# Attention backward, last pass: who requests the weight slabs of wq and wo, when, and into which buffers

## The chip, the cores and the metric

The kernel runs on one core of a Trainium2 chip. The metric is the device time of one execution, in microseconds (us); less is better. A core has a matrix engine (PE, TensorE, whose weight loads are listed as PEld), a vector engine (DVE, VectorE), an activation engine (ACT, ScalarE), a general one (POOL, GpSimd) and SyncE (SP), which here only requests transfers. Transfers between device memory and the on-chip buffers run on 16 transfer (DMA) engines. Each engine works through its own list of instructions in order. A transfer is requested by an instruction on one engine's list, and each requesting engine has its own queue of transfers.

## What is computed

The reference runs four layers on one token and then the gradient of all of it:

```python
x = x + _A_ref(_layernorm(x, axis=-1), A_k_cache, A_v_cache, A_wq, A_wo)
x = x + _B_ref(_layernorm(x, axis=-1), B_w1, B_b1, B_w2, B_b2)
x = x + _A_ref(_layernorm(x, axis=-1), A_k_cache, A_v_cache, A_wq, A_wo)
x = x + _B_ref(_layernorm(x, axis=-1), B_w1, B_b1, B_w2, B_b2)
```

`_A_ref` is attention with 32 query heads in 4 groups over a cache of 65536 positions of 128 numbers for each group (k and v, bf16, 67 MB each); q is x times wq (1024 x 4096), and the result goes through wo (4096 x 1024). `_B_ref` is a dense layer with a squared ReLU. Both attention layers use the same cache and weights. The outputs are the last x and the gradients with respect to x, k, v, wq, wo, w1, b1, w2 and b2. The gradients of k and v are as large as the caches: 134 MB that have to be written.

## The kernel before, in words

The kernel goes through the caches four times: two forward passes, a backward pass for the second attention layer, and a last pass that does the backward of the first attention layer and writes the gradients of k and v for both layers together. Only this last pass is touched.

**The last pass** (`attn_bwd4`) goes through 256 *items*, each of 8 columns of 128 cache positions: head groups 3, 2, 1, 0, 64 items each, in units of four items. A unit needs one 1 MB block of v and one of k. `pipeline` issues, for item i, the stages of different cache columns: v is turned by PE (`vT`, L1354), multiplied (`vS`, L1391), outer products make the gradients of v and k (`outer16`, PE at L1435), which ACT or DVE copy into a store buffer (`evac`, L161 and L164), and k is multiplied (`k8`, L1466). At the end of each item `bg.step` lets a background job do one step.

**Background jobs.** A job is a generator. `Background.step` gives each item's one step to the first *urgent* job; if that one yields "wait", the *normal* jobs (outer products for the weight gradients) get the step. Urgent are six jobs that multiply a vector with the rows of a weight matrix for one head group: `g_dO` (with wo, for groups 2, 1, 0, before the group's first v block is used) and `g_dn` (with wq, for groups 3, 2, 1, after the group's end). Called dO2, dO1, dn3, dO0, dn2, dn1 here, in the order in which they run, they start at items 16, 72, 102, 136, 166 and 202 of the background's count. Each needs 8 rows of 1024 columns for every partition, in two *slabs* of 1 MB, each with four of the rows. `g_rowdots` first spreads the vector (four steps, `g_bcast_vec`, L568 and L570), and then does one row a step: DVE multiplies (L596), and ACT sums the row of the step before (L585). `slabs` requests a slab when the loop comes to it (L459), so the second one only after the first has been used; the job then yields "wait" four times ahead of the first slab's rows and eight times ahead of the second's. In the last pass ACT requests the slabs of wq and SP those of wo.

**Buffers.** The arena has 20 buffers of 1 MB. Eight hold the exponentials of both layers for four groups, and two of them come free at the end of each group (`E_done`). A set `RING` marks the buffers that are meant for stores: two at the start of the pass, up to `NRING` = 5 soon after, and two more at the end of each group. `take_one` gives a store (`fill` true) the ring buffer that has been free for longest, and a load or a slab the one outside the ring that has been free for longest. Which buffer is used is settled when the program is written; at run time a request waits on its engine until the last user of that buffer is done. Loads of k and v (`kv8`, L361, L366) are written at the item that first uses them, and requested by SP, which has nothing else to do and so runs ahead of the other engines as far as the buffers let it. Stores (L1441 and others) are requested by POOL.

What decides on a buffer is this:

```python
if PS["pass4"]:
    mine = [i for _, i in by_age if (i in RING) == fill]
    i = mine[0] if mine else by_age[0][1] if fill else by_age[-1][1]
    del FREE[i]
    return i
```

The functions that the change touches, and those that call them:

Of the kernel before, what the change touches and what calls it, by code (L numbers as in the profile page):

```python
# [10 lines left out]
BF = mybir.dt.bfloat16  # L11
F32 = mybir.dt.float32
ACTF = mybir.ActivationFunctionType
ALU = mybir.AluOpType
AX = mybir.AxisListType
PSUM = bass.MemoryType.PSUM
P = 128
# [3 lines left out]
def kernel(  # L21
# [24 lines left out]
    nc = tc.nc  # L46
# [6 lines left out]
    R = HQ // G  # L53
    F = B_w1.shape[1]
    DC, FC = D // P, F // P
# [10 lines left out]
    TLEAD = 2  # L66
    STORE_STEPS = 5
    WAIT_STEPS = 5
    NSLOT = 12
    NWT = 6  # L70
    NKEEP = [8, 7, 7]
    NRING = 5
# [9 lines left out]
    PS = {}  # L82
# [62 lines left out]
    def add_load(act=0.0, dve=0.0, pe=0.0):  # L145
        load["act"] += act
        load["dve"] += dve
        load["pe"] += pe
# [289 lines left out]
    def f_rows_of(W):  # L438
        return W.rearrange("(s p j) n -> p s j n", p=P, j=4)

    def slabs(name, load, nk, kper, ncols, ahead=1, flat=False):
        pend = deque()
        ks = deque(range(0, nk, kper))

        def fetch():
            k = ks.popleft()
            i = None
            if ks and flat and NOW["wide"] and not odd_one():
                i = take_pair()
            if i is None:  # L450
                kn = min(kper, nk - k)
                sl = Slot(name)
            else:
                kn = min(2 * kper, nk - k)
                ks.popleft()
                sl = Slot(name, at=i, both=True)
            v = sl.t[:, 0:kn * ncols].rearrange("p (k n) -> p k n", n=ncols)
            queue = nc.scalar if PS["pass4"] and name == "s_wq" else nc.sync
            queue.dma_start(out=v, in_=load(k, kn))  # L459
            pend.append((k, kn, sl, v))  # L460

        def gen():
            while ks or pend:
                while ks and len(pend) < ahead:
                    fetch()
                k, kn, sl, v = pend.popleft()
                for kk in range(kn):
                    NOW["slab"] = sl
                    yield k + kk, v[:, kk, :]
                sl.over = True  # L470
                if not sl.users:
                    sl.free()
        g = gen()
        g_fetch = [fetch for _ in range(ahead)]
        return g, g_fetch
# [5 lines left out]
            f()  # L481
        return g

    def wq_slabs(g, ahead=1):
        v = rows_of(A_wq)
        return slabs("s_wq", lambda k, kn: v[:, k:k + kn, g * 1024:(g + 1) * 1024], DC, 4, 1024, ahead, True)

    def wo_slabs(g, ahead=1):
        v = rows_of(A_wo)
        return slabs("s_wo", lambda k, kn: v[:, g * R + k:g * R + k + kn, :], R, 4, 1024, ahead, True)  # L490

    def wo_runs(g):

        v = A_wo[g * 1024:(g + 1) * 1024, :].rearrange("(p k) n -> p k n", k=8)
        return slabs("s_wo", lambda k, kn: v[:, k:k + kn, :], R, 4, 1024, 1, True)[0]

    def w1_slabs(ahead=1):
        v = rows_of(B_w1)
# [58 lines left out]
    def g_bcast_vec(vcol, nj):  # L557
        pt = ps_mv([nj, P], F32)
        nc.tensor.transpose(pt[:, :], vcol, ident_f[:, :])
        yield  # L560
        rows = tmp.tile([32, P], BF, name="bc_rows")
        nc.vector.tensor_copy(out=rows[0:nj, :], in_=pt[:, :])
        vbc = mvs.tile([P, nj * P], BF, name="vbc", tag="vbc", bufs=1)
        yield
        for j0 in range(0, nj, 4):
            pg = ps_gg() if PS["pass4"] else ps_tr([P, 512], F32)
            for jj in range(4):
                nc.tensor.matmul(pg[:, jj * P:(jj + 1) * P], lhsT=ident_b[0:nj, j0 + jj:j0 + jj + 1].to_broadcast([nj, P]),  # L568
                                 rhs=rows[0:nj, :], start=True, stop=True)
            nc.scalar.copy(out=vbc[:, j0 * P:(j0 + 4) * P], in_=pg[:, 0:512])  # L570
            add_load(act=0.6)
            yield
        return vbc

    def g_rowdots(slab_it, nk, vcol, nj, finish, name):
        n = nj * P
        y = vec.tile([P, nk], F32, name=name)
        nc.gpsimd.memset(y[:], 0.0)
        vbc = None
        due = None  # L580
        steps = 8 if PS["pass4"] else WAIT_STEPS

        def total(t, kc):
            def f():
                nc.scalar.activation(out=t[:, :], in_=t[:, :], func=ACTF.Copy, accum_out=y[:, kc:kc + 1])  # L585
            return f
        for kc, slab in slab_it:
            if vbc is None:
                vbc = yield from g_bcast_vec(vcol, nj)
                for _ in range(steps - WAIT_STEPS + 1):  # L590
                    yield "wait"
            elif kc % 4 == 0:
                for _ in range(steps):
                    yield "wait"
            t = mvs.tile([P, n], BF, name="mv_t", tag="mv_t", bufs=2)
            nc.vector.tensor_tensor(out=t[:, :], in0=slab, in1=vbc[:, :], op=ALU.mult)  # L596
            add_load(dve=0.1 + n * 0.00054, act=0.42 + n * 0.00083)
            if due is not None:
                due()
            due = total(t, kc)  # L600
            yield
        due()
        yield
        r = finish(y[:, :])
        if r is not None:
            yield from r
        yield
# [308 lines left out]
    def gsl(g):  # L916
        return slice(g * R, (g + 1) * R)
# [10 lines left out]
    def g_wo(L, xacc, g, ps=ps_bg, it=None):  # L928
        def fin(p):
            nc.vector.tensor_tensor(out=xacc[:], in0=xacc[:], in1=p, op=ALU.add)  # L930
        if it is not None:
            yield from g_mv(it, R, 8, lambda kc: L["oTb"][:, g * R + kc:g * R + kc + 1], ps, fin)
            return
        each = tmp.tile([P, R, 8], BF, name="run_each", bufs=1)
        nc.vector.tensor_tensor(out=each[:, :, :], in0=L["oTb"][:, gsl(g)].unsqueeze(2).to_broadcast([P, R, 8]),
                                in1=eighth[:, :].unsqueeze(1).to_broadcast([P, R, 8]), op=ALU.mult)
        yield
        pt = ps_mv([P, R, 8])
        nc.tensor.matmul(pt[:, :, :].rearrange("p r k -> p (r k)"), lhsT=to_runs[:, :, :].rearrange("p a b -> p (a b)"),
                         rhs=each[:, :, :].rearrange("p r k -> p (r k)"), start=True, stop=True)  # L940
        yield
        own = tmp.tile([P, 8, R], F32, name="run_own", bufs=1)
        nc.vector.tensor_tensor(out=own[:, :, :], in0=pt[:, :, :].rearrange("p r k -> p k r"),
                                in1=M8[:, :].unsqueeze(1).to_broadcast([P, 8, R]), op=ALU.mult)
        oruns = tmp.tile([P, 8], F32, name="run_o")
        nc.vector.tensor_reduce(out=oruns[:], in_=own[:, :, :], axis=AX.X, op=ALU.add)
        orunb = tmp.tile([P, 8], BF, name="run_ob")
        nc.vector.tensor_copy(out=orunb[:], in_=oruns[:])
        yield
        yield from g_mv(wo_runs(g), R, 8, lambda kc: orunb[:, kc:kc + 1], ps, fin)  # L950


    def dO_finish(L, g):
# [18 lines left out]
    def g_dO(L, dx, g):  # L972
        def fin(y):
            each = tmp.tile([P, R, 8], F32, name="run_own", bufs=1)
            nc.vector.tensor_tensor(out=each[:, :, :], in0=y.unsqueeze(1).to_broadcast([P, R, 8]),
                                    in1=M8[:, :].unsqueeze(2).to_broadcast([P, R, 8]), op=ALU.mult)
            yield
            pt = ps_mv([P, R, 8], F32)
            nc.tensor.matmul(pt[:, :, :].rearrange("p r k -> p (r k)"), lhsT=from_runs[:, :, :].rearrange("p a b -> p (a b)"),
                             rhs=each[:, :, :].rearrange("p r k -> p (r k)"), start=True, stop=True)  # L980
            yield
            own = tmp.tile([P, R, 8], F32, name="run_own", bufs=1)
            nc.vector.tensor_tensor(out=own[:, :, :], in0=pt[:, :, :], in1=eighth[:, :].unsqueeze(1).to_broadcast([P, R, 8]), op=ALU.mult)
            back = tmp.tile([P, R], F32, name="run_o")
            nc.vector.tensor_reduce(out=back[:], in_=own[:, :, :], axis=AX.X, op=ALU.add)
            yield
            yield from dO_finish(L, g)(back[:, :])
        yield from g_rowdots(wo_runs(g), R, dx[:], DC, fin, "%s_dO%d" % (L["name"], g))


    def dn_finish(dn, first):
        def fin(y):
            if first:
                nc.vector.tensor_copy(out=dn[:], in_=y)
            else:
                nc.vector.tensor_tensor(out=dn[:], in0=dn[:], in1=y, op=ALU.add)
        return fin

    def g_dn(L, dn, g, first):
        yield from g_rowdots(wq_slabs(g)[0], DC, L["dqT"][:, gsl(g)], R, dn_finish(dn, first), "%s_dn%d" % (L["name"], g))  # L1000


    ACT_KT = (3, 13, 15)
# [1054 lines left out]
```

## Time and profile before

| | before |
|---|---|
| runs, median (lowest to highest of 3) | 1934.7 us (1932.66 to 1939.24) |
| profiled execution, its own time | 1936.54 us |
| its span, first to last instruction | 1934.7 us |
| bytes moved, mean rate over the span | 787.62 MB, 407 GB/s |
| busy share of the span: PE, DVE, ACT, POOL | 82%, 61%, 54%, 7% |
| 1 MB stores: requests, median from issue to landing | 149, 15.2 us |
| 1 MB slabs of wq by ACT: requests, median to landing | 8, 25.3 us |

The time and the span of the profiled execution differ by 1.8 us, which lie around the first and the last instruction. The profile lists, for each engine, what it was busy with, how long it sat idle and which instruction or transfer ended the wait; for the transfer engines, what they moved in each stretch of time. "Idle before" is the idle time just before an instruction. A request is on SP's, ACT's or POOL's list, and its landing is when the last byte has arrived.

### The profile page before, as it was taken

What the parts mean: (1) busy time and instruction counts of PE and PEld (TensorE: products, weight loads), DVE (VectorE), ACT (ScalarE), POOL (GpSimd) and SP (SyncE); (2) the same over time, 40 slices, a digit from 0 to 9 for tenths busy, and PEclk for the clock granted to TensorE, in tenths of its full rate; (3) what the DMA queues carried; (4) which work ended last, traced back from release to release, by engine and by line L of the source; (5) the groups of instructions that cost most, each with busy time, mean ns of one, the idle gap of its engine ahead of it and who ended that gap; (6) DMA issues with size and microseconds to landing.
All of it is one profiled execution on the core that took longest, in us unless ns stands there. A gap on an engine that the chain in (4) does not pass through costs nothing. (4 is left out here: it accounts for less than half of the span.)

```text
span 1934.7 us, 66770 instructions
## 1 busy us (share of the span) xinstructions
PE 1595.9 (82%) x30099; PEld 1303.7 (67%) x30099; DVE 1171.8 (61%) x2448; ACT 1044.5 (54%) x1619; POOL 143.4 (7%) x325
## 2 busy tenths in 40 slices
PE   6878788688778878978787888888978979789796
PEld 6878778678777778877777885555555555456463
DVE  5655555255555554645454576777867777667685
ACT  3434333345333545445363465666867677667676
POOL 0000000000000000000000002111211111111111
PEclk9989998799999998999899999898988889788896
DMA  9999999999999999999999997999999999999997
GB/s 394 426 428 424 427 429 416 403 420 415 428 425 428 429 414 327 376 426 429 425 426 422 404 366 285 425 424 386 424 425 423 424 402 407 393 403 416 421 419 301
DMA packets 107148, 787.62 MB, mean 407 GB/s; under 512 B 9440, under 2 KB 16622, under 8 KB 42222
## 3 DMA queue, kind: packets, MB, share of 16 engines
q1 hardware_dynamic: 78558, 609.26, 76.2%
q0 software_dynamic: 24080, 165.70, 20.5%
q10 hardware_dynamic: 4224, 8.39, 1.1%
q8 instruction: 235, 3.85, 0.7%
q14 instruction: 51, 0.42, 0.1%
HBM read 617.62 MB, written 165.69 MB: 405 GB/s over the span
## 5 line engine op out<-in xcount | busy, mean ns | idle before, releaser
L164 DVE COPY kt<-ps_tr 128x1024 bf16<-128x1024 bf16 x736 | 504.9, 688 | 434.6 <-PE ps_tr L1031 240.3
L161 ACT CAST arena<-ps_gg 128x1024 bf16<-128x1024 f32 x457 | 444.4, 1012 | 204.1 <-PE ps_gg L1435 136.3
L1031 PE MATMUL ps_tr<-ident_b,arena 128*128 128x128 bf16 x3840 | 312.4, 227 | 49.7 <-DMA arena<-in_A_k_cache_dram 37.0
L161 ACT COPY kt<-ps_tr 128x1024 bf16<-128x1024 bf16 x180 | 188.3, 1051 | 190.7 <-PE ps_tr L1225 108.9
L164 DVE CAST arena<-ps_gg 128x1024 bf16<-128x1024 f32 (+2 forms) x186 | 222.1, 1194 | 88.5 <-PE ps_gg L1435 51.1
L1031 PEld LDWEIGHTS <-arena 128*128 128x128 bf16 x3840 | 235.3, 102 | 58.6 <-DMA arena<-in_A_k_cache_dram 39.6
L1132 PE MATMUL ps_acc<-arena 128*128 128x64 bf16 (+4 forms) x4096 | 204.2, 196 | 46.4 <-DMA arena<-in_A_v_cache_dram 29.4
L1435 PE MATMUL ps_gg<-GG,xt 64*128 64x512 bf16 x1024 | 216.8, 420 | 19.5 <-ACT arena L161 8.8
L1354 PE MATMUL ps_tr<-ident_b,arena 128*128 128x128 bf16 x1824 | 181.2, 235 | 30.3 <-DMA arena<-in_A_v_cache_dram 16.4
L1049 PE MATMUL ps_sc<-L_qpad,kt 128*128 128x64 bf16 (+7 forms) x3584 | 183.5, 194 | 17.9 <-issue 10.9
L1114 ACT ACTIVATE arena<-S_sb,L_negm 128x128 bf16<-128x128 f32 x256 | 165.1, 1005 | 60.3 <-DVE L_negm L1099 60.3
L1225 PE MATMUL ps_tr<-ident_b,arena 128*128 128x128 bf16 x2032 | 161.7, 224 | 40.7 <-DMA arena<-in_A_v_cache_dram 39.0
L1132 PEld LDWEIGHTS <-arena 128*128 128x128 bf16 x4096 | 159.4, 101 | 52.4 <-DMA arena<-in_A_v_cache_dram 33.0
L1354 PEld LDWEIGHTS <-arena 128*128 128x128 bf16 x1824 | 120.7, 105 | 88.4 <-issue 68.7
L1049 PEld LDWEIGHTS <-kt 128*128 128x128 bf16 x3584 | 153.3, 100 | 21.8 <-issue 11.7
L1225 PEld LDWEIGHTS <-arena 128*128 128x128 bf16 x2032 | 122.6, 100 | 46.8 <-DMA arena<-in_A_v_cache_dram 41.3
L1466 PEld LDWEIGHTS <-arena 128*128 128x128 bf16 x2048 | 91.1, 101 | 63.1 <-DMA arena<-in_A_k_cache_dram 32.2
L1114 ACT ACTIVATION_READ_ACCUMULATOR arena<-S_sb,L_negm 128x1 f32 x256 | 128.0, 500 | 0.0
L1391 PEld LDWEIGHTS <-kt 128*128 128x128 bf16 x1824 | 85.2, 102 | 50.3 <-issue 48.7
L1391 PE MATMUL ps_sc<-DOB,kt 128*128 128x64 bf16 (+3 forms) x1824 | 118.2, 198 | 0.1
L1466 PE MATMUL ps_acc<-X,arena 128*128 128x64 bf16 (+3 forms) x1536 | 94.8, 197 | 26.3 <-DMA arena<-in_A_k_cache_dram 26.3
L585 ACT ACTIVATE mv_t<-mv_t 128x1024 bf16<-128x1024 bf16 x96 | 102.0, 1064 | 21.6 <-DVE mv_t L596 21.5
(319 smaller groups left out, 2102.8 us busy)
## 6 DMA issues: line engine op xcount, KB each, us to landing
arena<-in_A_k_cache_dram SPq DMA_DIRECT2D x82, 2048.0 KB, 21.4
arena<-in_A_v_cache_dram SPq DMA_DIRECT2D x79, 2048.0 KB, 20.7
out_dram<-arena POOLq DMA_DIRECT2D x149, 1024.0 KB, 15.2
arena<-in_A_v_cache_dram SPq DMA_DIRECT2D x84, 1024.0 KB, 12.6
arena<-in_A_k_cache_dram SPq DMA_DIRECT2D x84, 1024.0 KB, 12.8
arena<-in_A_wo_dram SPq DMA_DIRECT2D x22, 1024.0 KB, 13.9
arena<-in_B_w_dram SPq DMA_DIRECT2D x21, 1024.0 KB, 10.0
arena<-in_A_wq_dram SPq DMA_DIRECT2D x7, 2048.0 KB, 25.4
```

The costliest lines, as they stand in the source:

```text
L161: nc.scalar.copy(out=out, in_=in_)
L164: nc.vector.tensor_copy(out=out, in_=in_)
L585: nc.scalar.activation(out=t[:, :], in_=t[:, :], func=ACTF.Copy, accum_out=y[:, kc:kc + 1])
L1031: nc.tensor.transpose(pt[:, i, :], kb8[:, i, :], ident_b[:, :])
L1049: nc.tensor.matmul(state["ps_s"][:, s:s + w, :].rearrange("p a b -> p (a b)"), lhsT=kt[:, i, :], rhs=L["qpad"][:, g, 0:w, :].rearrange("p ...
L1114: nc.scalar.activation(out=E(p, g, c0, SU)[:, :, h], in_=S[:, h, :], func=ACTF.Exp, bias=L["negm"][:, g, su, h:h + 1], scale=SCALE, accum_ ...
L1132: nc.tensor.matmul(ps_o[:, 0:w, :], lhsT=vb8[:, i, :], rhs=E(p, g, c, w), start=(c % SU == 0), stop=(c % SU == SU - 1), skip_group_check=True)
L1225: nc.tensor.transpose(pt[:, i, :], vb8[:, i, :], ident_b[:, :])
L1354: nc.tensor.transpose(pt[:, i, :], vb8[:, i, :], ident_b[:, :])
L1391: nc.tensor.matmul(state["ps_dp"][:, s:s + w, :].rearrange("p a b -> p (a b)"), lhsT=vt[:, i, :], rhs=DOB[:, g, 0:w, :].rearrange("p a b - ...
L1435: nc.tensor.matmul(pg[:, 512 * h:512 * h + 512], lhsT=xt[64 * h:64 * h + 64, j1 // 8 + m, :], rhs=gg[64 * h:64 * h + 64, :, :].rearrange(" ...
L1466: nc.tensor.matmul(ps_dq[:, 0:w, :].rearrange("p a b -> p (a b)"), lhsT=kb8[:, i, :], rhs=X[:, s:s + w, :].rearrange("p a b -> p (a b)"), ...
```

## The change

In the last pass, a job asks for its first slab in its first step, for the second one five steps later, and then yields "wait" ten times before the first row; both slabs are held together. ACT requests the slabs of wo too. From the time when `RING` has at least seven buffers, the slabs go into ring buffers instead of those that the loads use. In the other passes nothing changes. `NRING` stays 5.

```diff
+    SLAB_STEPS = 10
...
-    def slabs(name, load, nk, kper, ncols, ahead=1, flat=False):
+    def slabs(name, load, nk, kper, ncols, ahead=1, flat=False, ring=False):
...
-                sl = Slot(name)
+                sl = Slot(name, ring and len(RING) >= NRING + 2)
...
-            queue = nc.scalar if PS["pass4"] and name == "s_wq" else nc.sync
+            queue = nc.scalar if PS["pass4"] else nc.sync
...
-    def g_rowdots(slab_it, nk, vcol, nj, finish, name):
-        n = nj * P
+    def g_dot(slab, vbc, y, kc, due):
+        t = mvs.tile([P, 1024], BF, name="mv_t", tag="mv_t", bufs=2)
+        nc.vector.tensor_tensor(out=t[:, :], in0=slab, in1=vbc[:, :], op=ALU.mult)
+        add_load(dve=0.65, act=1.27)
+        while due:
+            due.popleft()()
+
+        def total():
+            nc.scalar.activation(out=t[:, :], in_=t[:, :], func=ACTF.Copy, accum_out=y[:, kc:kc + 1])
+        due.append(total)
+
+    def rowdots(slabs_of, g, nk, vcol, nj, finish, name):
+        assert nj * P == 1024
         y = vec.tile([P, nk], F32, name=name)
         nc.gpsimd.memset(y[:], 0.0)
-        vbc = None
-        due = None
-        steps = 8 if PS["pass4"] else WAIT_STEPS
...
-        for kc, slab in slab_it:
-            if vbc is None:
-                vbc = yield from g_bcast_vec(vcol, nj)
-                for _ in range(steps - WAIT_STEPS + 1):
+        due = deque()
+        if PS["pass4"]:
+            slab_it, fetch = slabs_of(g, 2, True)
+            fetch[0]()
+            vbc = yield from g_bcast_vec(vcol, nj)
+            yield "wait"
+            fetch[1]()
+            for _ in range(SLAB_STEPS):
+                yield "wait"
+            for kc, slab in slab_it:
+                g_dot(slab, vbc, y, kc, due)
+                yield
+        else:
+            slab_it, _ = slabs_of(g)
+            vbc = None
+            for kc, slab in slab_it:
+                if vbc is None:
+                    vbc = yield from g_bcast_vec(vcol, nj)
                     yield "wait"
-            elif kc % 4 == 0:
-                for _ in range(steps):
-                    yield "wait"
...
+                elif kc % 4 == 0:
+                    for _ in range(WAIT_STEPS):
+                        yield "wait"
+                g_dot(slab, vbc, y, kc, due)
+                yield
...
-        yield from g_rowdots(wo_runs(g), R, dx[:], DC, fin, "%s_dO%d" % (L["name"], g))
+        yield from rowdots(wo_runs, g, R, dx[:], DC, fin, "%s_dO%d" % (L["name"], g))
...
-        yield from g_rowdots(wq_slabs(g)[0], DC, L["dqT"][:, gsl(g)], R, dn_finish(dn, first), "%s_dn%d" % (L["name"], g))
+        yield from rowdots(wq_slabs, g, DC, L["dqT"][:, gsl(g)], R, dn_finish(dn, first), "%s_dn%d" % (L["name"], g))
```

More of the change, by code (lines that the diff above doesn't have):

```diff
@@ L482, in prefetch, with wq_slabs @@
         return g
-    def wq_slabs(g, ahead=1):
+    def wq_slabs(g, ahead=1, ring=False):
         v = rows_of(A_wq)
-        return slabs("s_wq", lambda k, kn: v[:, k:k + kn, g * 1024:(g + 1) * 1024], DC, 4, 1024, ahead, True)
+        return slabs("s_wq", lambda k, kn: v[:, k:k + kn, g * 1024:(g + 1) * 1024], DC, 4, 1024, ahead, True, ring)
     def wo_slabs(g, ahead=1):
@@ L490, in wo_slabs, with wo_runs @@
         return slabs("s_wo", lambda k, kn: v[:, g * R + k:g * R + k + kn, :], R, 4, 1024, ahead, True)
-    def wo_runs(g):
+    def wo_runs(g, ahead=1, ring=False):
         v = A_wo[g * 1024:(g + 1) * 1024, :].rearrange("(p k) n -> p k n", k=8)
-        return slabs("s_wo", lambda k, kn: v[:, k:k + kn, :], R, 4, 1024, 1, True)[0]
+        return slabs("s_wo", lambda k, kn: v[:, k:k + kn, :], R, 4, 1024, ahead, True, ring)
     def w1_slabs(ahead=1):
@@ L577, in g_rowdots @@
+    def rowdots(slabs_of, g, nk, vcol, nj, finish, name):
+        assert nj * P == 1024
         y = vec.tile([P, nk], F32, name=name)
         nc.gpsimd.memset(y[:], 0.0)
-        vbc = None
-        due = None
-        steps = 8 if PS["pass4"] else WAIT_STEPS
[L583 to L586, printed above, removed]
-        for kc, slab in slab_it:
-            if vbc is None:
-                vbc = yield from g_bcast_vec(vcol, nj)
-                for _ in range(steps - WAIT_STEPS + 1):
-                    yield "wait"
-            elif kc % 4 == 0:
-                for _ in range(steps):
-                    yield "wait"
[L595 to L601, printed above, removed]
@@ L602, in g_rowdots @@
-        due()
+        due = deque()
[16 more added lines that the diff above has]
+                    vbc = yield from g_bcast_vec(vcol, nj)
+                    yield "wait"
+                elif kc % 4 == 0:
[3 more added lines that the diff above has]
+                yield
@@ L603, in g_rowdots @@
+        due.popleft()()
         yield
@@ L949, in g_wo @@
         yield
-        yield from g_mv(wo_runs(g), R, 8, lambda kc: orunb[:, kc:kc + 1], ps, fin)
+        yield from g_mv(wo_runs(g)[0], R, 8, lambda kc: orunb[:, kc:kc + 1], ps, fin)
     def dO_finish(L, g):
```

## The prediction

> **What bounds the kernel now.** The change touches the last pass alone (1165 us to the end), so I read stretches of it, not the page's averages. First the page's rows by slice:
>
> ```profile
> DMA  9999999999999999999999997999999999999997
> GB/s 394 426 428 424 427 429 416 403 420 415 428 425 428 429 414 327 376 426 429 425 426 422 404 366 285 425 424 386 424 425 423 424 402 407 393 403 416 421 419 301
> ```
>
> From slice 26 on the transfer engines are full at about 424 GB/s: the pass is bound by bytes, and the change moves no byte more or less. Time can be won only where the rate dips. Cut at the dips (columns: stretch, length, then busy us of PE, PEld, DVE, ACT and POOL, PE clock, DMA share, GB/s):
>
> ```profile
> 1200.00:1300.00 100.00, 84.98 (x1081) 53.63 (x1080) 75.32 (x134) 69.91 (x83) 20.64 (x39) 0.90 1.01 422
> 1300.00:1330.00 30.00, 25.86 (x301) 15.96 (x300) 19.80 (x37) 18.45 (x20) 4.35 (x8) 0.77 0.94 362
> 1330.00:1590.00 260.00, 222.65 (x2803) 140.73 (x2804) 192.22 (x347) 188.54 (x228) 46.82 (x89) 0.89 1.01 423
> 1590.00:1610.00 20.00, 18.80 (x287) 12.95 (x286) 16.72 (x40) 15.38 (x20) 3.03 (x5) 0.95 0.91 343
> ...
> 1680.00:1700.00 20.00, 19.74 (x225) 11.91 (x222) 15.47 (x28) 17.25 (x21) 2.67 (x5) 0.81 0.90 313
> ...
> 1740.00:1750.00 10.00, 9.72 (x118) 5.79 (x119) 7.79 (x11) 7.40 (x9) 2.21 (x4) 1.00 0.98 368
> ```
>
> Against 423, a dip costs length x (423 - rate)/423: 4.3 us at 1300-1330, 3.8 at 1590-1610, 5.2 at 1680-1700, 1.3 at 1740-1750. Each follows a stall of the engines, during which the rate held: transfers already asked for ran on, then buffers were not freed in time, and PE, busy 85% even on average, catches up slowly. What stalled before 1680 is in VectorE's timeline:
>
> ```profile
> 1664.97 0.68 DVE L1412 TENSOR_TENSOR X<-ps_sc,arena 128x512 bf16<-128x512 f32 x1
> 1677.98 0.69 DVE L596 TENSOR_TENSOR mv_t<-arena,vbc 128x1024 bf16<-128x1024 bf16 x1 [12.32 <-issue]
> ```
>
> The 12.32 us have no releaser named, but L596 reads a slab: the second half of a wq list, which ScalarE requested at 1652.0 and which landed 25.9 us later, at 1677.9. Eight items lay between request and use, here only 13 us. Before 1590 PE waited 8.3 us (1578.8 to 1587.1) for a v block; SyncE issued no load between 1577.95 and 1595.58. SyncE's waits from 1200 us on say why:
>
> ```profile
> SPq L361 <- PE ps_acc L1466: 340.6, 44, 17.7
> SPq L361 <- PE ps_tr L1354: 195.6, 38, 15.1
> ```
>
> SyncE waits nearly always for a buffer that PE is still reading: how early a load can go out is set by how many buffers the loads share.
>
> **The change part by part.** One item is one step of Background; 8 weight loads of L1466 are an item, and items 19 to 263 start at 1198.7 and 1898.7: 2.87 us each. Six lists use L596: dO2 (from item 16), dO1 (72), dn3 (102), dO0 (136), dn2 (166), dn1 (202).
>
> *Requests earlier.* Counting the yields: before, each half is used 8 items after its request. After, the first dot comes 15 items after the first request and the fifth 14 after the second. 14 items are 40 us on average; the longest slab landing from 1200 us on is 25.9. The 12.3 us stall goes, and the 2.1 us one at 1473.7 too. What is late next is a load or a store buffer, below. Gain: the dip behind it, 5.2 us, not 12.3, since the rate held at 424 while VectorE stood.
>
> *Arithmetic.* 48 multiplications (680 ns) and 48 sums (1069 ns) stay; a list has 30 steps instead of 31. Zero.
>
> *wo requests from SyncE to ScalarE.* Six requests of 0.37 us: 2.2 us of ScalarE, which idles about 30% of the pass; cover gone, 2.2 us. SyncE loses six of 0.33 us, nothing to it. What counts is the wait for the buffer ahead of a request. SyncE had these:
>
> ```profile
> SPq L459 <- PE ps_sc L1391: 17.3, 1, 17.3
> ...
> SPq L459 <- PE ps_acc L1466: 15.8, 3, 5.5
> ...
> SPq L459 <- DVE mv_t L596: 10.0, 1, 10.0
> ```
>
> A wait of this kind on ScalarE would hold up its evacuations (L161) and sums (L585), queued behind it, and PE behind those. The Trainium skill ("DMA: Bandwidth & Descriptors", section "Anatomy of one DMA — SWDGE (gpsimd) path") says that transfer engines never wait on semaphores: the sequencer that issues does. The trace agrees (the 17.3 us stand on SyncE); by that rule alone the waits move with the requests, 17.3 + 15.8 + 10.0 us for wo, and at 5.2 us lost for 12.3 of stall, as at 1680, the sum below would be 18 us higher. ScalarE comes to its request in the order of the program, though, when a buffer freed items ago has been read; its own eight requests show it:
>
> ```profile
> L459 ACTq EVENT_SEMAPHORE  x10: 17/28/38, 1411.9 to 1857.8; - x10
> ```
>
> 28 ns, no wait. New is that a buffer may hold a store not yet written out. The nearest row is evacuations waiting for that:
>
> ```profile
> ACT arena L161 <- DMA out_dram<-arena: 22.2, 10, 4.7
> ```
>
> Six of the ten ring requests fall on a buffer last used by a store, 7 to 12 items earlier, that is 20 to 34 us; stores land in 15.5 us (median). Bounds 0 and 4.7 us each; I take 0.
>
> *Buffers.* I followed take_one and give_slot through the pass, in program order. RING is 7 from item 68, so dO1 and all later lists take store buffers, as the edit says. For a load I count the items between the freeing of its buffer and its use (what SyncE can run ahead), for a store the items since its buffer was given back. Loads, before to after, mean: items 72-102 8.1 to 10.2; 102-128 8.2 to 11.1; 128-166 7.5 to 9.9; 166-192 6.5 to 9.0; 192-230 7.1 to 9.3; the least in all of it rises from 5 to 9. Stores: 9.7 to 7.6; 9.8 to 7.6; 11.9 to 9.8; 13.1 to 8.8; 13.6 to 12.0.
> - Loads: two to four items are 6 to 11 us, against the 8.3 us wait before 1590 (a list held a load buffer there). Bounds 0 and the dips behind late loads, 3.8 + 1.3 = 5.1. I take 5.1: nowhere from 72 on does a lead stay at 5.
> - Stores in the second group: both slabs out leave five buffers, as the first group had. There, in its most crowded part (age mean 6.4, least 3), ScalarE waited 4.5 us until 1302.1 for a store, and 4.3 us were lost at 1300-1330; in items 72-102 of before (9.7, least 5) a wait of 4.7 until 1352.2 cost nothing. 7.6 lies between: bounds 0 and 4.3, I take half, 2.2.
> - First group: dO2 still takes load buffers, now two at once in items 21 to 35; leads fall from 7.1 to 5.7 (least 6 to 5). Bounds 0 (the rate was 422 there, stores queued) and 3.8 (the dip at lead 5). Half: 1.9.
>
> **Sum**: -5.2 - 5.1 + 2.2 + 1.9 = -6.2 us. The profiled execution took 1936.5 us, 1934.7 of it span, so it would take 1930.3; it lies 1.8 above the median of the runs, 1934.7, whose forecast is 1928.5. By 0.3% (5.8 us), about what a measurement of this kernel can tell, that is 1928.9: just faster.
>
> **Rivals.**
> *All won.* No give-back: -10.3, 1924.4. For: the counted leads; the idle store buffers of later groups (9 to 11). Against: five store buffers in the second group.
>
> *No change.* The pass is bound by bytes, the lost 10 us come from bunching, and the next shortage (a group's start, PE's catching up) makes dips of the same size elsewhere: 1934.7, give or take 4. For: dips exist with no slab near them (1300-1330). Against: only a stall of over 8 us, or one that met tight buffers, left a dip. The Trainium skill has a rule on this side ("DMA: Bandwidth & Descriptors", section "Issuing engines are not separate DMA queues"): requests from several engines share the same transfer engines, so moving wo saves issue time alone. The trace agrees that a third queue adds no rate (1610-1680, a slab on ScalarE's queue: 424; 1330-1590: 423), so nothing is booked for the move itself.
>
> *Store buffers short: slower.* With both slabs taken from RING, stores wait for their buffer on ScalarE and VectorE, as at 1297-1302, and each such wait costs the 4.3 us of 1300-1330. Place: items 77-95 and 106-121, then 141-159 and 170-188. The gain without stores is 10.3 - 1.9 = 8.4, so two such waits eat it and four make 4 x 4.3 - 8.4 = +8.8: 1943.5. For: ages of 5 in 72-128. Against: from 128 on mean ages stay at 8.8 or above, over the 6.4 where it cost.
>
> **Numbers.** Forecast 0.50 (own range 1924 to 1933; 0.30 below 1928.9, 0.20 within 0.3%); all won 0.17; no change 0.15; store buffers 0.18 (0.15 slower by 0.3%, 0.03 within). Faster 0.47, same 0.38, slower 0.15. Range 1921 to 1942: down past the all-won case by the runs' own spread (1932.7 to 1939.2), up through most of the slower rival.
>
> **What the changed profile would show.** L596's idle of 12.3 us gone; a request by ScalarE for each of the 12 list slabs with no idle of ScalarE before it; no dip at the place of 1680-1700 and a smaller one at 1590-1610; SyncE's waits in the same total but PE's waits for k and v shorter; "out_dram<-arena" waits of ScalarE above 22.2 us, mostly in the second group. I am wrong if new dips of 4 us or more follow store waits in items 77-121 or load waits in items 21-40, or if ScalarE's requests wait for microseconds.

## The result, and the profile after

The change made the kernel slower: 1957.4 us median (1956.81 to 1958.35, 5 runs) against 1934.7 (1931.54 to 1941.48, 5 runs) of the kernel before beside it, a ratio of 1.0114, 95% interval 1.0095 to 1.0134. The forecast was 1928.5 and the range ended at 1942. The profiled execution took 1957.48 us, its span is 1955.7, at the same granted clock as before (0.907 and 0.909).

The page's row of rates by slice, after the change (slice 26 begins at 1271 us, where the last pass is well under way):

```profile
GB/s 395 426 426 425 428 429 415 396 416 424 429 425 427 428 417 329 403 426 428 425 428 414 393 296 338 366 384 411 404 398 400 424 421 395 424 424 346 421 421 284
```

Before, slices 26 to 31 stood at 423 to 425 but for one of 386; now slices 26 to 30 lie between 384 and 411, and 395 and 346 follow. Cut into four stretches (stretch, length, then busy us of PE, PEld, DVE, ACT and POOL, PE clock, DMA share, GB/s), first of the kernel before, then of the changed one (from 1800 to 1900 us both ran at 420 GB/s):

```profile
1200.00:1340.00 140.00, 119.92 (x1493) 75.30 (x1491) 104.25 (x188) 96.12 (x112) 27.15 (x52) 0.88 1.00 409
1340.00:1500.00 160.00, 136.99 (x1732) 87.14 (x1731) 118.31 (x213) 117.78 (x144) 28.64 (x54) 0.89 1.01 424
1500.00:1650.00 150.00, 133.17 (x1700) 84.07 (x1699) 112.23 (x214) 109.63 (x131) 27.37 (x52) 0.90 1.00 411
1650.00:1800.00 150.00, 127.73 (x1591) 81.38 (x1591) 104.61 (x170) 100.07 (x121) 26.78 (x51) 0.84 1.00 405
```

```profile
1200.00:1340.00 140.00, 105.23 (x1327) 67.28 (x1326) 92.00 (x160) 84.37 (x98) 23.32 (x43) 0.83 0.96 382
1340.00:1500.00 160.00, 137.18 (x1645) 85.62 (x1642) 116.55 (x206) 110.81 (x133) 27.35 (x52) 0.86 0.99 398
1500.00:1650.00 150.00, 124.95 (x1661) 80.86 (x1661) 110.81 (x218) 103.93 (x127) 26.94 (x50) 0.91 1.01 422
1650.00:1800.00 150.00, 124.51 (x1602) 79.51 (x1599) 102.22 (x162) 99.34 (x119) 25.52 (x49) 0.87 0.96 391
```

Call length x (424 - rate)/424 the *loss* of a stretch; it is the measure used below. Before it is 4.9, 0, 4.6 and 6.7 us; after 13.9, 9.8, 0.7 and 11.7. So 9 us are lost in the **first group** (1200 to 1340, where dO2 runs) and 11 in the **later groups**; 2 more lie behind 1900 us.

**Later groups.** The stall of 12.3 us on VectorE is gone: L578, which multiplies now, waits for no slab anywhere. ScalarE stands instead. Its waits for stores, before and after (1200 to 1915 us; line, what it waited for, us in total, times, longest):

```profile
ACT arena L161 <- DMA out_dram<-arena: 18.7, 9, 4.7
```

```profile
ACT arena L162 <- DMA out_dram<-arena: 64.3, 12, 23.8
```

ScalarE's timeline shows the longest of them (start, us, what, and in brackets the idle time before and what ended it; ACTq is its sequencer, which issues the request):

```profile
1738.38 1.01 ACT L162 CAST arena<-ps_gg 128x1024 bf16<-128x1024 f32 x1 [1.60 <-PE ps_gg L1448]
1762.75 0.38 ACTq L460 DMA_DIRECT2D arena<-in_A_wq_dram  x1
1763.17 1.93 ACT L162 CAST arena<-ps_gg 128x1024 bf16<-128x1024 f32 x2 [23.78 <-DMA out_dram<-arena]
```

The wait is written beside the evacuation at 1763.17, but the request stands ahead of that evacuation and goes out in the same moment: it is the request that waits, and the evacuation stands in line behind it. The store it waited for left the same buffer at 1733.2 and landed at 1762.6. PE pays next, in its own timeline:

```profile
1764.23 0.61 PE L1526 MATMUL ps_gg<-arena,rowa 2*128 2x512 bf16 x2 [18.33 <-ACT arena L162]
```

The trace has six such *holds*, at 1328, 1397, 1478, 1571, 1641 and 1763 us: 1.3 + 8.1 + 8.8 + 9.4 + 10.0 + 23.4 = 61 us of ScalarE. The first ends with an instruction of VectorE (L1425). Each of the other five, 60 us, ends with the landing of the store that had used the buffer (issued and landed: 1381.9 and 1396.7, 1460.0 and 1478.0, 1553.0 and 1571.2, 1625.9 and 1640.4, 1733.2 and 1762.6). The row of the requests' semaphore waits, 28 ns in the median and at most 38 before, tells it too (duration ns, least/median/most; of the hold of 23.4 us it has only the last moment, and the idle time above shows the rest):

```profile
L460 ACTq EVENT_SEMAPHORE  x14: 17/38/10619, 1196.8 to 1870.1; - x14
```

**First group.** PE waits for k, from 1200 to 1340 us, before and after:

```profile
PE ps_acc L1466 <- DMA arena<-in_A_k_cache_dram: 5.1, 1, 5.1
```

```profile
PE ps_acc L1479 <- DMA arena<-in_A_k_cache_dram: 25.0, 4, 6.8
```

### The profile page after: what moved, and what is told of

Its sections match the earlier page's. It is cut to its first block, busy times and chain, and to the rows that moved or that the text cites. A ratio compares the mean times of both kernels' runs of the same rounds, so it can differ in the third digit from the quotient of the medians.

```text
span 1955.7 us, 66765 instructions
## 1 busy us (share of the span) xinstructions
PE 1589.8 (81%) x30099; PEld 1302.9 (67%) x30099; DVE 1175.3 (60%) x2447; ACT 1041.3 (53%) x1620; POOL 143.4 (7%) x325
## 5 line engine op out<-in xcount | busy, mean ns | idle before, releaser
L162 ACT CAST arena<-ps_gg 128x1024 bf16<-128x1024 f32 (+2 forms) x456 | 442.3, 1015 | 234.6 <-PE ps_gg L1448 126.0
L1448 PE MATMUL ps_gg<-GG,xt 64*128 64x512 bf16 x1024 | 213.4, 418 | 47.1 <-ACT arena L162 31.4
L1448 PEld LDWEIGHTS <-xt 64*128 64x128 bf16 x1024 | 64.6, 94 | 90.3 <-issue 55.0
L1292 PE MATMUL ps_acc<-dsT,arena 128*128 128x64 bf16 (+7 forms) x2048 | 102.9, 194 | 13.1 <-DMA arena<-in_A_k_cache_dram 7.3
## 6 DMA issues: line engine op xcount, KB each, us to landing
arena<-in_A_v_cache_dram SPq DMA_DIRECT2D x84, 1024.0 KB, 13.3
arena<-in_A_k_cache_dram SPq DMA_DIRECT2D x84, 1024.0 KB, 10.8
```

The lines of the kernel that those rows point to most:

```text
L162: nc.scalar.copy(out=out, in_=in_)
L1292: nc.tensor.matmul(ps_dq[:, 0:w, :].rearrange("p a b -> p (a b)"), lhsT=kb8[:, i, :], rhs=dsT[:, s:s + w, :].rearrange("p a b -> p (a b)") ...
L1448: nc.tensor.matmul(pg[:, 512 * h:512 * h + 512], lhsT=xt[64 * h:64 * h + 64, j1 // 8 + m, :], rhs=gg[64 * h:64 * h + 64, :, :].rearrange(" ...
```

## The experiments

Why does the request stand where the store has not landed, if its buffer was given back 7 to 12 items earlier? Because the last pass is not laid out by hand: the framework's scheduler puts each engine's list in an order of its own. I compared the order of the lists with the order in which the source writes the instructions. In the changed kernel the twelve slab requests of the six jobs on ScalarE stand 3 to 17 items *ahead* of their written places (the two of dO1 17 and 3, of dO0 14 and 7), five of the six held ones close behind the store of the buffer that they take. The multiplications stand 2 to 9 items ahead, the sums about 10. In the kernel before they stand ahead too, and so do the requests: the first of dn3 is written at item 102, which starts at about 1437 us (83 items of 2.87 us after 1198.7), and went out at 1412.7. Its slab lay in a load buffer, though, and no request there waited more than 38 ns. An instruction can be tied to its written place: `keep` below stands for `tc.keep_in_program_order`, which puts it behind the one written just before it on its engine. The experiments take these in turn. Every loss is from one profiled execution; those of e3, e4, e5 and e13 (1956.1, 1956.8, 1943.6 and 1959.8 us) lie furthest from their medians, 6 to 10 us. Where dO2 is the same, in before, e8 and e9, the first group's losses lie between 4.7 and 6.2, so a difference of 1.5 us says little. Medians are of 4 to 12 runs; the median of the kernel before beside them was 1934.2 (e1 to e4), 1937.5 (e5 to e8), 1935.9 (e9 to e12), 1935.7 (e13 to e15) and 1934.6 (e16, e17, e20).

| | median, us | ratio to before, 95% interval | loss 1200-1340 | loss 1340-1900 |
|---|---|---|---|---|
| before | 1934.7 | | 4.9 | 12.4 |
| the change | 1957.4 | 1.0114 [1.0095, 1.0134] | 13.9 | 23.1 |
| e1: requests in order | 1964.0 | 1.0156 [1.0130, 1.0183] | 15.6 | 26.1 |
| e2: dO2 as before | 1943.7 | 1.0049 [1.0033, 1.0065] | 6.7 | 17.4 |
| e3: no store buffers | 1966.2 | 1.0167 [1.0120, 1.0213] | 12.2 | 21.6 |
| e4: e1 + e2 | 1951.0 | 1.0086 [1.0054, 1.0119] | 6.5 | 30.5 |
| e5: e4 + uses in order | 1937.6 | 1.0007 [0.9982, 1.0031] | 15.5 | 4.5 |
| e6: before + uses in order | 1948.2 | 1.0053 [1.0029, 1.0078] | 10.5 | 13.7 |
| e7: before + wo by ScalarE | 1948.6 | 1.0066 [1.0039, 1.0092] | 13.3 | 17.4 |
| e8: before + store buffers | 1959.9 | 1.0107 [1.0071, 1.0143] | 6.2 | 38.2 |
| e9: e5, dO2 wholly as before | 1931.6 | 0.9988 [0.9971, 1.0005] | 4.7 | 5.7 |
| e10: change, dO2 by SyncE | 1953.5 | 1.0084 [1.0060, 1.0109] | 6.2 | 25.9 |
| e11: change, dO2 one slab at a time | 1954.5 | 1.0093 [1.0075, 1.0111] | 12.5 | 21.7 |
| e12: e7 + wo requests in order | 1954.8 | 1.0100 [1.0082, 1.0118] | 13.7 | 18.4 |
| e13: e7 + loads in order | 1949.4 | 1.0065 [1.0042, 1.0089] | 12.9 | 17.7 |
| e14: before + loads in order | 1935.0 | 0.9995 [0.9974, 1.0016] | 4.0 | 10.8 |
| e15: change, requests and uses in order | 1949.7 | 1.0061 [1.0041, 1.0080] | 23.9 | 8.1 |
| e16: e7 + products in order | 1975.7 | 1.0210 [1.0182, 1.0238] | 17.4 | 42.3 |
| e17: before + products in order | 1972.1 | 1.0188 [1.0149, 1.0227] | 12.8 | 46.7 |
| e20: change, in order from dO1 on, products in order | 1944.1 | 1.0046 [1.0025, 1.0067] | 13.7 | 11.0 |

### The later groups: the order of requests and uses

**e1_in_order**: the requests alone.

```diff
-            queue.dma_start(out=v, in_=load(k, kn))
+            d = queue.dma_start(out=v, in_=load(k, kn))
+            if ring:
+                keep(d)
```

> The changed kernel with each list's slab requests kept, on ScalarE, at the place where they are written (in the changed kernel the request stands 3 to 17 items ahead of that place, right behind the store of the buffer that it takes). Theory A, ScalarE is held at requests that were moved up to unfinished stores (61 us at six of ten ring requests): the holds fall under 10 us in all, the DMA loss after 1340 us from 22 to about 6 us, the time from 1957.4 to about 1941 us (1936 to 1946); the first group's loss (13 us at 1200 to 1300) stays. Theory B, the stores have too few buffers, and whoever comes first waits: the same wait moves to the evacuations, the time stays within 1952 to 1962.

The holds fell from 61 us to 0, as they should. The time did not fall. VectorE waits for slabs now (1340 to 1900 us):

```profile
DVE mv_t L580 <- DMA arena<-in_A_wq_dram: 51.3, 4, 15.4
```

With the request at its place and the multiplication still 2 to 9 items ahead of its own, the lead of 14 items is no longer there. Both answers on record missed: the order of the requests alone is not enough.

**e2_first_group_old**: dO2 asks for one slab at a time, eight items ahead and by SyncE, as before; all else is the change. **e3_load_buffers**: `Slot(name)` for all slabs, so that no store buffer is used. **e4_both**: e1 and e2 together.

```diff
-            queue = nc.scalar if PS["pass4"] else nc.sync
+            queue = nc.scalar if PS["pass4"] and (ring or name == "s_wq") else nc.sync
...
-        if PS["pass4"]:
+        if PS["pass4"] and len(RING) >= NRING + 2:
...
-                    yield "wait"
+                    for _ in range(4 if PS["pass4"] else 1):
+                        yield "wait"
...
-                    for _ in range(WAIT_STEPS):
+                    for _ in range(8 if PS["pass4"] else WAIT_STEPS):
```

```diff
-                sl = Slot(name, ring and len(RING) >= NRING + 2)
+                sl = Slot(name)
```

> The changed kernel with dO2, the only list of the first group, as before: slabs one after the other, eight items ahead, wo by SyncE. Theory C, two load buffers fewer in the first group cost 9 us there: 1200 to 1300 us is back at 420 GB/s, the time falls to about 1948 us (1945 to 1951). Rival: the first group's loss comes from the other order of instructions, not from the buffers: the time stays within 1954 to 1960.

> The changed kernel with all slabs in load buffers, none in the ring. Theory A: ScalarE is no longer held by stores (under 3 us at requests), but theory C's price, about 9 us a list with two load buffers out, comes in all six lists: slower than the changed kernel, about 1975 us (1960 to 1985). Theory B: stores have their buffers back, only the loads are shorter: 1940 to 1950 us.

> Requests kept at their place on ScalarE, and dO2 as before. Theories A and C together: 1930 us (1925 to 1937), what the prediction had without the two losses. Theory B: about 1948 us.

e2 won 13.7 us on the change, more than the 9 of the first group. e3 has no holds, so they do come from the store buffers, but PE then waits 75.4 us for k (19 times, 1165 to 1915 us; before 31.4 in 8): two load buffers held for some 20 items are no better than the holds. e4 has neither the first group's loss nor holds, and VectorE waits 59.2 us for slabs: the loss in the later groups is 30.5, and the time is far from the 1930 us of the two theories together.

**e5_all_in_order**: e4 with the uses tied as well.

```diff
-        nc.vector.tensor_tensor(out=t[:, :], in0=slab, in1=vbc[:, :], op=ALU.mult)
+        d = nc.vector.tensor_tensor(out=t[:, :], in0=slab, in1=vbc[:, :], op=ALU.mult)
+        if PS["pass4"]:
+            keep(d)
...
-            nc.scalar.activation(out=t[:, :], in_=t[:, :], func=ACTF.Copy, accum_out=y[:, kc:kc + 1])
+            a = nc.scalar.activation(out=t[:, :], in_=t[:, :], func=ACTF.Copy, accum_out=y[:, kc:kc + 1])
+            if PS["pass4"]:
+                keep(a)
```

> Like e4 (requests at their place, dO2 as before), and the multiplications on VectorE and the sums on ScalarE are kept at their place too; in e4 the multiplications still stand 2 to 9 items ahead of it and VectorE waits 59 us for slabs. Theory D, the item counts of the source hold only if request and use both stay where they are written: neither ScalarE at requests nor VectorE at slabs waits more than 5 us in all, the DMA loss after 1340 us is under 10 us (e4: 30), the time about 1932 us (1926 to 1938). Rival, the store buffers are too few once the stalls are gone: the evacuations' waits for stores grow past 40 us and the time stays within 1944 to 1953.

The later groups lose 4.5 us instead of 30.5: VectorE waits for no slab, and ScalarE was held at two requests alone, 2.6 and 2.9 us. The first group lost 15.5 here though it was as before but for its uses, which now stand late; my reading is that they keep load buffers longer.

**e6_before_uses_in_order** puts the uses alone in order in the kernel before.

> The kernel before with only the multiplications and sums of the lists kept at their place. Theory D: the 12.3 and 2.1 us waits for slabs go, and with them the 5.2 us dip: 1929 us (1926 to 1932). Rival: the pass is bound by bytes and the loss turns up elsewhere: 1933 to 1937.

Both answers fell. The waits for slabs went, as expected, all but 1.3 us, but PE waits longer for v (1165 to 1915 us; before 16.4 us for v and 31.4 for k). The slabs of that kernel lie in load buffers and are now held longer, which is the likely reason:

```profile
PE ps_tr L1358 <- DMA arena<-in_A_v_cache_dram: 40.7, 12, 10.4
PE ps_acc L1470 <- DMA arena<-in_A_k_cache_dram: 31.1, 11, 5.8
```

**e8_before_ring**: the kernel before, one slab at a time, but from store buffers from the second group on; wo's queue stays SyncE's.

```diff
-                sl = Slot(name)
+                sl = Slot(name, ring and PS["pass4"] and len(RING) >= NRING + 2)
```

> The kernel before with only the buffers changed: from the second group on the slabs, one at a time, eight items ahead, by SyncE and ScalarE as before, come from the ring. Theory A: ScalarE (wq) and SyncE (wo) are held behind stores, over 15 us on ScalarE: 1940 to 1950 us. Rival: only the count of free buffers matters, one more for loads, one fewer for stores: at or below 1934.

The store buffers alone bring the holds: 54.8 us at five wq requests of ScalarE, and 38.2 us lost; the time is 22 us above the kernel before beside it, more than the theory's 1940 to 1950. So it is not the second slab and not the queue of wo that make them.

```profile
ACT arena L161 <- DMA out_dram<-arena: 69.8, 12, 17.4
```

**e9_order_but_first_old**: e5, with dO2 wholly as before.

```diff
-        if PS["pass4"]:
+        if PS["pass4"] and len(RING) >= NRING + 2:
             keep(d)
...
-            if PS["pass4"]:
+            if PS["pass4"] and len(RING) >= NRING + 2:
                 keep(a)
```

> Like e5, but dO2 is left as the kernel before has it, its multiplications and sums free to move too; the five later lists keep requests and uses at their place. In e5 the losses of 1340 to 1900 us were 4.5 us and those of 1200 to 1340 15.5 (before: 12.4 and 4.9). Theory C+D: the first is kept, the second falls to about 6: some 9 us faster than e5, 1927 to 1931 with before at 1935. Rival: the first group's losses change from order to order by chance, and nothing is gained: 1935 to 1939.

Its stretches from 1340 us on:

```profile
1340.00:1500.00 160.00, 137.35 (x1732) 86.26 (x1731) 115.29 (x208) 112.66 (x130) 28.77 (x53) 0.88 1.01 419
1500.00:1650.00 150.00, 133.39 (x1754) 85.97 (x1752) 117.78 (x218) 111.93 (x139) 28.74 (x52) 0.90 1.01 424
1650.00:1800.00 150.00, 130.35 (x1656) 82.56 (x1656) 112.02 (x173) 109.38 (x134) 27.29 (x52) 0.89 1.00 414
```

419, 424 and 414 are losses of 1.9, 0 and 3.5 us, where the kernel before lost 0, 4.6 and 6.7. No request of ScalarE waits longer than 1.7 us:

```profile
L460 ACTq EVENT_SEMAPHORE  x12: 17/38/1702, 1383.9 to 1846.2; - x12
```

This is the change as its source reads, for dO1 and all later jobs, and the lowest median of all kernels here: 1931.6 us, just above the 1927 to 1931 on record and 4 below the kernel before, though the interval of the ratio, 0.9971 to 1.0005, does not exclude no difference.

### The first group: the queue of wo

**e7_before_wo_scalar**: the kernel before with one line changed.

```diff
-            queue = nc.scalar if PS["pass4"] and name == "s_wq" else nc.sync
+            queue = nc.scalar if PS["pass4"] else nc.sync
```

> The kernel before with only the queue of wo changed to ScalarE's; buffers of the loads, one slab at a time, eight items as before. The readers of these buffers are PE's, so ScalarE is held under 5 us at its requests: no change, 1932 to 1938. Rival: the change of queue itself costs: above 1940.

It fell. No request holds ScalarE, and yet the first group loses 13.3 us, as in the change, and PE waits 53.6 us for k where it waited 31.4 (1165 to 1915 us).

**e10_do2_sync** and **e11_do2_scalar_one** take the change's dO2 apart: two slabs early, but by SyncE; and one slab at a time, but by ScalarE (the edit of e2 without its first line).

```diff
-            queue = nc.scalar if PS["pass4"] else nc.sync
+            queue = nc.scalar if PS["pass4"] and (len(RING) >= NRING + 2 or name == "s_wq") else nc.sync
```

> The changed kernel with only the queue of dO2's two requests back on SyncE; both are still requested early and held together in load buffers. Theory C (two load buffers held cost the first group): no change, 1954 to 1961, PE waits for k over 20 us. Rival E (the queue: on ScalarE's queue the slabs pass the loads, and they stand elsewhere in the order): 1942 to 1948, as e2.

> The changed kernel with dO2's slabs one after the other and eight items ahead as before, but requested by ScalarE. Theory C: 1942 to 1947, as e2. Rival E (the queue): 1953 to 1959, as the changed kernel.

6.2 against 12.5 us: the loss goes with the queue. The second load buffer costs 6.2 - 4.9 = 1.3, no more than kernels with the same dO2 differ. The time of e10, 1953.5 us, hit neither answer: of the 7.7 us that the first group got back the later groups lost 2.8 again.

**e12_before_wo_in_order**: e7 with wo's requests tied to their written places.

```diff
+            if PS["pass4"] and name == "s_wo":
+                keep(d)
```

> e7 (the kernel before with wo requested by ScalarE, 11 us slower) with these six requests kept where they are written; in e7 they stand 4 to 21 items ahead. Theory F, moved up they take their load buffers too early: 1934 to 1940, PE's waits for k from 53 us to about 31. Rival E, the third queue itself costs: 1945 to 1951.

13.7 us: that they stand early on ScalarE's list is not the reason.

**e13_loads_in_order_wo_scalar**, **e14_loads_in_order_wo_sync**: with wo off SyncE's list, the loads of k and v stand in another order there from the fifth load of the group on. Both kernels tie them to the written order (e14, with wo by SyncE, its wo requests too).

```diff
-                nc.sync.dma_start(out=sl.t.rearrange("p (j d) -> p j d", d=DH), in_=half(KVIN[t], g, hb))
+                d = nc.sync.dma_start(out=sl.t.rearrange("p (j d) -> p j d", d=DH), in_=half(KVIN[t], g, hb))
+                if PS["pass4"]:
+                    keep(d)
```

> e7 (the kernel before with the wo slabs of the last pass requested by ScalarE) with SyncE's loads of k and v in the last pass kept in the written order. Theory E1 (the loss of the first group is the order that the loads take on SyncE's list once wo is off it): the stretch 1200 to 1340 us loses the same here as in e14, within 2 us. Theory E2 (the third queue shares the transfer engines with the loads of k): 8 us or more above e14 there.

> The kernel before with SyncE's loads of k and v and its wo requests in the last pass kept in the written order: the control for e13. Theory E1: its loss from 1200 to 1340 us is that of e13. Theory E2: about 5 us there, as before, and 8 or more below e13. Time 1932 to 1945 us, since nothing else changes.

The stretch from 1200 to 1340 us, and PE's waits for k in it, first e13, then e14:

```profile
1200.00:1340.00 140.00, 109.39 (x1409) 69.55 (x1408) 96.90 (x174) 87.36 (x102) 24.31 (x47) 0.88 0.97 385
```

```profile
PE ps_acc L1468 <- DMA arena<-in_A_k_cache_dram: 19.0, 6, 6.4
```

```profile
1200.00:1340.00 140.00, 123.33 (x1505) 76.59 (x1503) 105.20 (x191) 97.41 (x113) 27.68 (x53) 0.85 1.00 412
```

```profile
PE ps_acc L1470 <- DMA arena<-in_A_k_cache_dram: 3.8, 2, 3.4
```

385 and 412 are losses of 12.9 and 4.0. The order of the loads is not the reason either (E1 falls), and the difference, 8.9 us, is what E2 expected. But the transfers of k took no longer in e13 (issues from 1190 to 1345 us, median us to landing, first e13, then e14; 12.8 in the change and 12.0 in the kernel before):

```profile
arena<-in_A_k_cache_dram SPq DMA_DIRECT2D x12, 1024.0 KB, 9.7
```

```profile
arena<-in_A_k_cache_dram SPq DMA_DIRECT2D x15, 1024.0 KB, 10.2
```

And the two kernels differ in one thing more. I counted, on PE's list, the matmuls into the outer products' buffer (`ps_gg`) that stand before the 300th product into `ps_acc` (counted from the end of the third pass; it is about the 130th of those of the last pass, which need k). It is 114 to 116 in the kernel before, e2, e4, e8, e9, e10 and e14, which lose 4.0 to 6.7 us in the first group, and 76 to 104 in the change, e1, e3, e7, e11, e12, e13 and e15, which lose 12.2 to 23.9. (e5 and e6 have 114, and lose 15.5 and 10.5; they have dO2's uses late. And in the second set the loss does not follow the count: e7 with 80 lost 13.3, e12 with 100 lost 13.7.) So moving wo to another queue also made the scheduler place PE's products with k earlier, with 12 to 40 matmuls of 0.21 us less ahead of them (216.8 us for 1024 of L1435 in the kernel before), 2 to 8 us.

**e16_products_late_wo_scalar**, **e17_products_late_wo_sync**: e7 and the kernel before with that product tied, which makes the two lists of PE alike in the first part of the pass (150 in both). **e20_change_products_late**: the same tie in the change, with requests and uses in order from dO1 on.

```diff
-                nc.tensor.matmul(ps_dq[:, 0:w, :].rearrange("p a b -> p (a b)"), lhsT=kb8[:, i, :],
+                m = nc.tensor.matmul(ps_dq[:, 0:w, :].rearrange("p a b -> p (a b)"), lhsT=kb8[:, i, :],
...
+                if i == 0:
+                    keep(m)
```

> e7 (the kernel before with wo requested by ScalarE) with the first product of every eight key blocks (the one that needs k) kept at its written place on TensorE. In the lists of e7, e13 and the changed kernel this product stands some 40 matmuls further ahead of its written place than in those of the kernel before and e14 (126 to 138 ahead against 86, a mean over the first half of the pass), so that 76 to 80 outer matmuls stand before the 300th product, against 116. Theory E3 (the order on TensorE's list, which the queue of wo changes, makes the loss of the first group): with both lists made alike by hand, the stretch 1200 to 1340 us loses the same in e16 and e17, within 2 us, and at most 6. Theory E2 (the third queue shares the transfer engines with the loads of k): e16 loses 8 us or more above e17 there.

> The kernel before with the same product kept at its written place on TensorE, wo on SyncE's queue: the control for e16. E3: its loss from 1200 to 1340 us is that of e16, within 2 us. E2: 8 us or more below e16. Its total I leave open from 1930 to 1950 us, since buffers of k are held longer.

> The change, dO2 as changed, with requests, multiplications and sums in the written order from the second group on (as e9) and the product that needs k kept at its written place. E3: the first group loses at most 6 us (the changed kernel 13.9), 1340 to 1900 us about 6 (e9 5.7), 1930 to 1936 us in all. E2: the first group still loses 12 to 15 us, 1938 to 1943 us.

From 1200 to 1340 us, e16, then e17:

```profile
1200.00:1340.00 140.00, 116.46 (x1313) 68.63 (x1312) 98.48 (x173) 91.51 (x106) 24.18 (x46) 0.80 0.93 372
```

```profile
1200.00:1340.00 140.00, 112.84 (x1331) 67.23 (x1329) 97.08 (x171) 92.58 (x107) 25.36 (x49) 0.84 0.96 385
```

PE waits for no k in this stretch in either, so it was that early product that met k too soon. But both lose more than they did (17.4 and 12.8; e17 took 1972.1 us where 1930 to 1950 was on record), it seems because blocks of k are now held longer: PE waits for v (7.4 us in three pieces in both); and they differ by 4.6 us, between the 2 of E3 and the 8 of E2. e20 lost 13.7 in the first group and 1944.1 us in all, just above what E2 named. Neither theory is borne out as stated.

**e15_change_in_order**: the change, dO2 as changed, with requests and uses of all six jobs in order (the edits of e1 and e5, so dO2's requests too, though the text on record ties them from the second group on).

> The change with requests from the second group on, multiplications and sums kept in the written order, and dO2 as changed. Theory D (the cost of groups two and on is the order in which requests and uses stand, not the change as written): under 6 us lost from 1340 to 1900 us (e5 lost 4.5, e9 5.7, the changed kernel 23); the first group still loses 12 to 16 us; 1936 to 1941 us in all. Rival: two load buffers held for 20 items by dO2, with uses no longer early, cost more: above 1943 us.

The later groups lose 8.1 us, against 23.1 in the change: more than the 6 on record, and still 15 of it gone. The first group loses 23.9, as the rival had it. That is near the sum of what the parts cost apart: 4.7 (e9), + 10.8 for dO2's uses in order (e5 against e9), + 9.0 for the change's dO2.

## Why the prediction was wrong

**"14 items are 40 us on average ... the 12.3 us stall goes"** was right: it went, and no other wait for a slab took its place. What it was worth could be had only in order: 1650 to 1800 us loses 3.5 us in e9 against 6.7 before, and the prediction had 5.2 of gain there.

**"ScalarE comes to its request in the order of the program ... Bounds 0 and 4.7 us each; I take 0"** is the step that failed, in size and in reason. The list of an engine is not the order of the program. The requests stood 3 to 17 items ahead, five of them had to wait for a store's landing, and that took 60 us, up to 23.4 each, not 4.7. The eight requests of 28 ns were no sign of order: they stood ahead of their places as well, and met load buffers that nobody used any more. The price: 23.1 us lost from 1340 to 1900 us, against 5.7 with order kept (e9), so some 17 us. The bound was taken from evacuations that wait for a store buffer; an evacuation takes the one that has been free for longest, so most of the landing is over when it comes, while a request that is moved up to the store has most of the landing ahead of it (14 to 29 us here).

The rule of the Trainium skill quoted there ("DMA: Bandwidth & Descriptors", section "Anatomy of one DMA — SWDGE (gpsimd) path"), that the issuing sequencer does the waiting, had the right side: by it the sum was 18 us higher, +12, and +22.7 was measured. It was not the three waits of SyncE that moved, though, but new ones, for stores.

The sign of it stood in the prediction's own lines. The slab requested at 1652.0 was wanted at 1665.7, "eight items" later and "here only 13 us"; at 2.87 us an item, eight are 23. The multiplication had been moved further ahead of its written place than the request. A count of items that disagrees with the clock is a reason to look at the lists.

**"Buffers. I followed take_one and give_slot ... in program order"** was right for a kernel that keeps that order, and for no other. The gains and give-backs of these steps and the stall's were -5.2 - 5.1 + 2.2 = -8.1 us of loss; e9 has 12.4 - 5.7 = 6.7 less. The rival "store buffers short" did not occur in that form: in e9 ScalarE's waits for store buffers are 23.5 us in 19 pieces from 1340 to 1900 us, the longest 4.4 (before 8.9 in 4), with nothing lost behind them but the 5.7.

**"First group ... half: 1.9"**: the mechanism costed there, two load buffers at once, measured 1.3 us (e10), not clear of none. What cost 8 to 9 us (e7, e11, e13 against e14, the change) was **"nothing is booked for the move itself"**. The support for that was the rate, 424 GB/s with a third queue in use. The rate under full load was the wrong row: moving six requests took 1937.5 to 1948.6 us (before to e7, one line), and with the loads in order 1935.0 to 1949.4 (e14 to e13). It came with other engines' lists laid out anew, and the transfers of k were not slower. The rule of the Trainium skill that several issuing engines share the same transfer engines, so that a move saves issue time alone ("DMA: Bandwidth & Descriptors", section "Issuing engines are not separate DMA queues"), was on that side too. As a forecast of the kernel's time it failed here, by those 11 to 14 us.

**What stays open**: how the 9 us divide between PE's order and something else that comes with the queue. e13 and e14 exclude the order of the loads, e12 the place of wo's requests; e16 and e17 leave 4.6 us with alike products, from one profile each, in kernels that lose more anyway. Whether requests from ScalarE cost k anything directly was not shown; the time of its transfers to landing does not say so (9.7 us in e13, 10.2 in e14).

The signs of being wrong that the prediction named came: requests of ScalarE that wait for microseconds, a new dip with load waits in about items 21 to 40 (1204 to 1261 us: 361 GB/s, before 425), and 9.8 us lost from 1340 to 1500 us, where two requests waited for stores.

## What to carry to other kernels

A lead counted in steps of the source holds only if the request *and* the use keep their places; where a scheduler lays out the lists, compare their order with the source's first, and tie both ends or neither (one end alone was worse: e1, e6). That paid where the slabs lie in store buffers; in load buffers both ends tied cost more (the first group of e15 lost 23.9 us, that of the change 13.9). A request on a compute engine's list into a buffer that a store has just left stops that engine until the store has landed; give it a place at least a landing later, as in e9, or, not tried here, an engine with nothing behind it. And moving a request to another queue is an edit of every list, so try it by itself before counting on what it frees.

## What the runs showed that was not expected

How long a 1 MB store takes to land depends on how many are under way: issues from 1700 to 1770 us, median us to landing, before and after:

```profile
out_dram<-arena POOLq DMA_DIRECT2D x11, 1024.0 KB, 13.0
```

```profile
out_dram<-arena POOLq DMA_DIRECT2D x9, 1024.0 KB, 28.6
```

The slow stores of the changed kernel were issued ahead of the longest hold, which begins at 1739.4 us: those from 1703.6 to 1735.6 took 24 to 29.5 us, and the first one behind it, at 1765.4, took 5.5. The store that the request waited for had five others ahead of it, and they landed 4 to 6 us apart. So the line of stores made the hold long, and not the hold the line; what had bunched them was not tested.

Also, a stop of 23.4 us on ScalarE and 18.3 on PE cost only some 10 us of transfers (1650 to 1800 us lost 11.7): the transfers that were already asked for ran on meanwhile (407 GB/s from 1739 to 1763 us, then 334 until 1800), as behind the 12.3 us stall of the kernel before.
